# Linear attention ahead of a Mish feed-forward: exponentials by sign in two tiles, num by sign within a bank, loads placed behind projections, first key unit over two pools

## The chip, the cores and the metric

One core of one Trainium2 chip. The metric is the device time of one execution in microseconds (us), taken as the median of several runs.

## The reference

Eight batches of eight heads, 576 tokens, head width 64. Queries and keys are projected to 128 features, the largest absolute value of each row is subtracted, and both signs go through an exponential. The attention is linear: keys and values are summed first, then the queries are multiplied by the sums. Its output is the input of a feed-forward layer with the Mish activation.

```python
def phi(x):
    proj = np.einsum('bhsd,df->bhsf', x, w_phi)
    proj = proj - np.max(np.abs(proj), axis=-1, keepdims=True)
    return np.concatenate([np.exp(proj), np.exp(-proj)], axis=-1)
q_p, k_p = (phi(q), phi(k))
kv = np.einsum('bhsf,bhsd->bhfd', k_p, v)
z = np.sum(k_p, axis=2)
num = np.einsum('bhsf,bhfd->bhsd', q_p, kv)
den = np.einsum('bhsf,bhf->bhs', q_p, z)[..., None] + 1e-06
...
h = x @ w_in
sp = np.where(h > 20.0, h, np.log1p(np.exp(np.minimum(h, 20.0))))
g = h * np.tanh(sp)
return (g @ w_out).astype(np.float32)
```

## The kernel before

The attention is cut into 36 units of 512 columns (a pair of heads at a time), for keys and for queries alike. The feed-forward weights are split meanwhile into high and low words, 16 pieces of them during the attention; the feed-forward itself (from about 272 us on) uses the split parts and seven products per 2x2 block of blocks.

All operations are entered into one list with a time that was written by hand, as `at(time, fn, unit)`, and the program is the list in the order of the times. The time of unit u is `base(u)`, and a beat is 7.341 in those units. The times set only the order in which each engine finds its instructions; the waits between engines follow from the tiles. The engines each work through their own instructions in order, and SyncE (SP) issues all transfers in order.

What a beat does, by engine:

- TensorE (PE): `q_num` (num, 64 records in the trace), `k_sum` (kvps, 64 or 80), `q_turn` (dt, 16 transposes of the centred query projection), `k_proj` (pp_k, 16), and `project_turn`, which mixes the query projection pp_q with the transposes xt0 and xt1 of a finished output x.
- ScalarE (ACT): `q_exp`, four exponentials that read the two dt banks and write e_q; two key exponentials in place; copies of xt, kv and of the denominators r; a cast for the weights.
- VectorE (DVE): row maxima m_k and m_q, the subtractions e_k and e_q, the reciprocal of r, x = num * r in two operations, and for a weight piece the word operations `shift`, `sign` and `scale` (L194, L198, L204).
- GpSimd (POOL): the rest of the weight split. Its `clamp` (L190) stands ahead of `shift`, its `low` (L219) behind `scale`.
- SP: per beat the store of xs (x_spill), the loads kraw, qraw, v and, on some beats, the words of a weight piece and the two spills of a split piece.

Results of PE land in two PSUM pools. `ps_a` holds two projections pp. `ps_b` has four banks that turn by tag: dt0, dt1, xt0, xt1, num0, num1 and kvps all take the next free one. A tile that takes a bank waits for the last reader of the tile that had it. A num bank is filled by 16 matmuls of two row halves: for each j and t, first the exponentials of one sign, then of the other. The query's tile e_q holds both signs (index s); the signed value s=0 overwrites the centred projection. Key and query tiles share one tag e with five buffers.

The first key unit (unit 0) is projected in two cuts, since its second half is loaded later.

Of the kernel before, what the change touches and what calls it, by code (L numbers as in the profile page):

```python
# [8 lines left out]
F32 = mybir.dt.float32  # L9
# [79 lines left out]
def attention_then_mish(ctx, tc, qT, kT, va, w_phi, w_in, w_out, w_out2, out):  # L89
# [200 lines left out]
    def project(raw, name, cuts=(0, 4)):  # L290

        parts = []
        ps = ps_a.tile([P, 2, 4, F], F32, tag="pp", name=f"pp_{name}")
# [32 lines left out]
    def center(parts, name):  # L326
        e = att.tile([P, 2, 2, 512], F32, tag="e", name=f"e_{name}", bufs=5)
        m = att.tile([P, 2, 4], F32, tag="m", name=f"m_{name}", bufs=4)
        to = e[:, :, 0, :].rearrange("p j (n f) -> p j n f", f=F)
# [4 lines left out]
        return e  # L334

# [33 lines left out]
    def k_center(n):  # L369
        k_live[n] = center(k_live.pop(n), f"k_{n}")  # L370
# [40 lines left out]
    def q_load(n):  # L411
        q_live[n] = att.tile([P, 512], F32, tag="qraw", name=f"qraw_{n}", bufs=3)
        nc.sync.dma_start(q_live[n], qT[n // 2, n % 2])
# [9 lines left out]
    def q_center(n):  # L423
        q_live[n] = center(q_live.pop(n), f"q_{n}")
# [7 lines left out]
    def q_sub(n):  # L432
        ps, m = q_live[n]
        e = att.tile([P, 2, 2, 512], F32, tag="e", name=f"e_q_{n}", bufs=5)
        nc.vector.tensor_tensor(e[:, :, 0, :].rearrange("p j (n f) -> p j n f", f=F), ps,
# [3 lines left out]
    def q_turn(n, j):  # L439
# [5 lines left out]
        for jj in range(2):  # L445
            for i in range(4):
                for h in range(2):
                    rows = slice(h * D, (h + 1) * D)
                    nc.tensor.transpose(turned[n, h][:, jj, i], e[rows, jj, 0, i * P:(i + 1) * P], ident[rows, rows])  # L449

    def q_exp(n, h):
        e, ps = q_live[n].rearrange("p j s (i h t) -> p s h j i t", h=2, t=D), turned.pop((n, h))
        for s in range(2):
            nc.scalar.activation(e[:, s, h], ps, AF.Exp, scale=2.0 * s - 1.0)  # L454

    def q_num(n):
        c, g = divmod(n, 2)
        es = q_live.pop(n)
        x = x_live[n] = att.tile([P, 2, 2, P], F32, tag="x", name=f"x_{n}", bufs=3)
# [381 lines left out]
    for u in range(NU):  # L841
# [4 lines left out]
        at(t + (LOAD_AT[0] if u >= LEAD else -11.1), k_load, u)  # L846
        at(t + (LOAD_AT[1] if u > LEAD else V_AT[u]), v_load, u)
# [74 lines left out]
    for i, pc in enumerate(pieces):  # L922
# [10 lines left out]
        if beat:  # L933
            clock = base(2 * i)
            load_at = clock - (15.0 if i > 3 else 13.4)
        at(load_at, weight_load, *pc)
        for delay, op in bits:
            if i == 2 and op in bits_of(bits, 2, 3):
                delay += STEP
            if i == 2 and op in bits_of(bits, 4):  # L940
# [6 lines left out]
        for j, (cost, op) in enumerate(sums):  # L947
# [3 lines left out]
            if pc[1] >= 2 and j in (high, len(sums) - 1):  # L951
                at(clock + (SPILL_AT[j > high and not quiet] if not beat else 1.2 if j == high else 5.25), spill, int(j > high))
# [163 lines left out]
```

## Time and profile before

| | us |
|---|---|
| median of 3 runs | 1009.7 |
| the runs | 1008.92, 1009.7, 1011.41 |
| the profiled execution, its own time | 1010.88 |
| its span in the profile | 1009.1 |
| PE busy in the span | 992.0 |
| DVE busy | 751.3 |
| ACT busy | 504.4 |
| POOL busy | 286.0 |

The profiled execution lies 1.2 us above the median. The attention ends at about 272 us. In the rows, a value in brackets at the end of a line is the idle time of the engine just ahead of it and what ended it; "issue" means that the profile shows nothing that it waited for. PE stands for matmuls and transposes, PEld for their weight loads.

### The profile page before, as it was taken

How to read it: one execution, taken by the hardware profiler on the slowest of the kernel's cores; microseconds unless marked ns; L12 is line 12 of the kernel's file. 1: busy time of each engine (PE TensorE's matmuls, PEld its weight loads, DVE VectorE, ACT ScalarE, POOL GpSimd, SP SyncE). 2: the span in 40 equal slices, each digit the busy share in tenths (PEclk: the TensorE clock that was granted, in tenths of full speed). 3: DMA queues.
4: the chain of work that ended last, by engine and by line, in shares of the span. 5: the costliest groups of instructions: out<-in, count | busy, mean ns of one | idle time of the engine just before them, and what ended most of it. 6: DMA issues, size and time to landing. Idle time of an engine off the chain costs nothing.

```text
span 1009.1 us, 28988 instructions
## 1 busy us (share of the span) xinstructions
PE 992.0 (98%) x12418; PEld 952.1 (94%) x12418; DVE 751.3 (74%) x1168; ACT 504.4 (50%) x904; POOL 286.0 (28%) x267
## 2 busy tenths in 40 slices
PE   8999999999999999999999999999999999999998
PEld 7989999899999999999999999999999999999998
DVE  7999899888557788879985675757575757575755
ACT  5878887787745446454453433333333333333332
POOL 0674455453505253456536010101010101010101
PEclk9999999999999999999999999999999999999999
DMA  6656577775697968898858996868686868686841
GB/s 209 210 184 197 181 234 240 248 247 177 234 384 295 325 245 308 297 327 284 291 201 284 351 346 218 314 220 312 220 314 222 311 222 311 224 309 223 309 168 73
DMA packets 111200, 259.02 MB, mean 257 GB/s; under 512 B 8672, under 2 KB 47328, under 8 KB 109024
## 3 DMA queue, kind: packets, MB, share of 16 engines
q1 hardware_dynamic: 111072, 257.17, 72.1%
q8 instruction: 98, 1.61, 0.7%
q14 instruction: 30, 0.25, 0.1%
HBM read 179.27 MB, written 77.86 MB: 255 GB/s over the span
## 4 chain that ended last, share of the span: by engine, by line
PE 91%; ACT 5%; issue 2%; POOL 1%; DVE 1%; DMA 0%; SPq 0%; DVEq 0%
PE h L580 36%; PE o L732 22%; PE o L709 15%; PE num L340 7%; PE kvps L340 6%; ACT e_q L454 3%; PE dt L449 2%; PE pp_k L300 1%; PE pp_q L309 1%; ACT e_k L374 1%; DMA kraw<-kT 0%; PE pp_q L300 0%; PE xt L491 0%; DVE e_k L332 0%; PE xt L315 0%
## 5 line engine op out<-in xcount | busy, mean ns | idle before, releaser
L580 PE MATMUL h<-xc,win 128*128 128x256 f32 x3024 | 380.4, 283 | 0.0
L580 PEld LDWEIGHTS h<-xc,win 128*128 128x128 f32 x3024 | 373.8, 192 | 4.4
L804 POOL TENSOR_TENSOR part<-part,du 128x512 f32<-128x512 f32 x18 | 23.4, 1297 | 425.8 <-DVE du L794 425.8
L732 PE MATMUL o<-wa,gh 128*128 128x256 f32 x720 | 130.7, 283 | 0.0
L732 PEld LDWEIGHTS o<-wa,gh 128*128 128x128 f32 x720 | 111.8, 192 | 0.0
L709 PE MATMUL o<-wout,gh 128*128 128x512 f32 x432 | 108.2, 392 | 0.0
L612 DVE TENSOR_TENSOR u<-h,u 128x512 f32<-128x512 f32 x72 | 49.5, 688 | 70.1 <-PE h L580 70.1
L732 PE MATMUL o<-wa,gl 128*128 128x256 f32 x360 | 100.7, 283 | 0.0
L732 PE MATMUL o<-wb,held 128*128 128x256 f32 x795 | 95.8, 281 | 0.2 <-DVE du L794 0.2
L732 PEld LDWEIGHTS o<-wb,held 128*128 128x128 f32 x795 | 94.9, 189 | 0.4 <-DVE du L794 0.4
L709 PEld LDWEIGHTS o<-wout,gh 128*128 128x128 f32 x432 | 77.7, 189 | 13.9
L454 ACT ACTIVATE e_q<-dt 128x512 f32<-128x512 f32 x144 | 74.3, 604 | 17.7 <-PE dt L449 17.5
L340 PE MATMUL kvps<-v,e_k 128*64 128x65 f32 (+1 forms) x2560 | 77.4, 222 | 2.4 <-issue 2.1
L340 PEld LDWEIGHTS num<-kv,e_q 128*64 128x64 f32 x2304 | 71.0, 137 | 8.6 <-ACT e_q L454 5.8
L340 PE MATMUL num<-kv,e_q 128*64 128x65 f32 x2304 | 76.2, 223 | 2.9 <-issue 0.9
L628 ACT ACTIVATE sb<-h 128x256 f32<-128x256 f32 x45 | 17.3, 384 | 119.4 <-PE h L580 85.6
L340 PEld LDWEIGHTS kvps<-v,e_k 128*64 128x64 f32 (+1 forms) x2560 | 72.4, 137 | 4.7 <-issue 2.7
L631 ACT ACTIVATE u<-u 128x768 f32<-128x768 f32 x45 | 38.1, 847 | 72.7 <-DVE u L612 72.7
L374 ACT ACTIVATE e_k<-e_k 128x1024 f32<-128x1024 f32 x64 | 67.7, 1057 | 11.5 <-DVE e_k L332 11.1
L667 ACT CAST gh<-sb 128x1024 fp32r<-128x1024 f32 x45 | 47.2, 1050 | 50.4 <-DVE sb L660 50.4
L732 PEld LDWEIGHTS o<-wa,gl 128*128 128x128 f32 x360 | 68.6, 192 | 0.0
L679 DVE TENSOR_TENSOR gl<-sb,gh 128x1024 fp32r<-128x1024 f32 x45 | 61.0, 1357 | 0.7 <-ACT gh L667 0.7
(111 smaller groups left out, 1614.2 us busy)
## 6 DMA issues: line engine op xcount, KB each, us to landing
win<-in_spill SPq DMA_DIRECT2D x44, 896.0 KB, 8.2
xc<-xc_spill SPq DMA_DIRECT2D x63, 512.0 KB, 5.9
xc_spill<-xc SPq DMA_DIRECT2D x56, 512.0 KB, 6.5
wa<-out_spill SPq DMA_DIRECT2D x29, 768.0 KB, 6.2
in_spill<-wst_in SPq DMA_DIRECT2D x24, 448.0 KB, 3.3
v<-va SPq DMA_DIRECT2D x32, 325.0 KB, 4.4
qraw<-qT SPq DMA_DIRECT2D x36, 256.0 KB, 4.0
x_spill<-xs SPq DMA_DIRECT2D x36, 256.0 KB, 3.0
```

Source lines behind the costliest of these rows:

```text
L340: nc.tensor.matmul(ps[rows], lhsT[:, rows], rhs[h], start=start, stop=stop, skip_group_check=True)
L374: nc.scalar.activation(e[:, :, s], e[:, :, 0], AF.Exp, scale=2.0 * s - 1.0)
L449: nc.tensor.transpose(turned[n, h][:, jj, i], e[rows, jj, 0, i * P:(i + 1) * P], ident[rows, rows])
L454: nc.scalar.activation(e[:, s, h], ps, AF.Exp, scale=2.0 * s - 1.0)
L580: nc.tensor.matmul(ps, w, x, start=(i in (0, 2) and m == 0), stop=(m == 5), skip_group_check=True)
L612: nc.vector.tensor_tensor(u[:, 0:3:2] if second(n) else u[:, 1:3], hy, u2.unsqueeze(1).broadcast_to([P, 2, CH]), op=ALU.add)
L631: nc.scalar.activation(u[:, 0:3], u[:, 0:3], AF.Mish)
L667: nc.scalar.copy(gh, u_live[n][4])
L679: nc.vector.tensor_tensor(gl, u_live[n][4], g_live[n]["h"].bitcast(F32), op=ALU.subtract)
L709: nc.tensor.matmul(o_live[s][tt], g[:, 2 * f + which, cols], wout[fp][:, f, k], start=(first and g is gh and f == k == 0), stop=(last and ...
L732: nc.tensor.matmul(ps, g, w, start=(start and k == 0), stop=(stop and k == 2), skip_group_check=True)
L804: nc.gpsimd.tensor_tensor(cross, cross, d_live[s, tau][0].unsqueeze(1).broadcast_to([P, 2, CH]), op=ALU.add)
```

## The change

The queries' exponentials go to two tiles: e0 (three buffers), in which the projection is centred and which then takes s=0 in place, and e1 (two buffers) for s=1. `q_exp` is now called per sign and not per dt bank: first both banks for s=0, then both for s=1. `q_num` runs over the sign outside j and t within a bank. The keys keep the tag e, now with three buffers; qraw and x have two in place of three.

The second cut of the first key unit is projected into two tiles of `ps_b`, one for each j, and centred by two pairs of VectorE operations.

In the table of times: a key load of unit u stands right behind the key projection of unit u-3, a query load right behind the query projection of unit u-2 (each takes the buffer that this projection frees); v loads stand 0.9 earlier, weight words of pieces 5 and on 22.994 ahead of their beat in place of 15.0; the second spill of a piece 3.3 in place of 5.25 behind; `shift` and `sign` of piece 3 one beat later, as those of piece 2; the query projection of unit 33 is 2.2 earlier.

```diff
     def project(raw, name, cuts=(0, 4)):
...
         for a, b in zip(cuts, cuts[1:]):
-            parts.append((a, b, ps))
+            if a:
+                by_j = [ps_b.tile([P, b - a, F], F32, tag="b", name=f"pp{j}_{name}") for j in range(2)]
+            else:
+                ps = ps_a.tile([P, 2, 4, F], F32, tag="pp", name=f"pp_{name}")
+                by_j = [ps[:, j, a:b] for j in range(2)]
+            parts.append((a, b, by_j if a else ps))
...
-                    nc.tensor.matmul(ps[:, j, n], src, w_phi2[rows], start=True, stop=True)
+                    nc.tensor.matmul(by_j[j][:, n - a], src, w_phi2[rows], start=True, stop=True)
...
+    def centered(n):
+        return att.tile([P, 2, 512], F32, tag="e0", name=f"e0_{n}", bufs=3)
...
+            if a:
+                for j in range(2):
+                    nc.vector.tensor_reduce(m[:, j, a:b], ps[j], axis=AX.X, op=ALU.max, apply_absolute_value=True)
+                    nc.vector.tensor_tensor(to[:, j, a:b], ps[j], m[:, j, a:b].unsqueeze(2).broadcast_to([P, b - a, F]),
+                                            op=ALU.subtract)
+                continue
...
-    def q_exp(n, h):
-        e, ps = q_live[n].rearrange("p j s (i h t) -> p s h j i t", h=2, t=D), turned.pop((n, h))
-        for s in range(2):
-            nc.scalar.activation(e[:, s, h], ps, AF.Exp, scale=2.0 * s - 1.0)
+    def q_exp(n, s):
+        if s:
+            q_live[n] = q_live[n], att.tile([P, 2, 512], F32, tag="e1", name=f"e1_{n}", bufs=2)
+        e = (q_live[n][1] if s else q_live[n]).rearrange("p j (i h t) -> p h j i t", h=2, t=D)
+        for h in range(2):
+            ps = turned.pop((n, h)) if s else turned[n, h]
+            nc.scalar.activation(e[:, h], ps, AF.Exp, scale=2.0 * s - 1.0)
...
         for i in range(2):
-            for j in range(2):
-                for t in range(2):
-                    r0 = (2 * c + t) * P
-                    for s in range(2):
-                        halves(num_live[n, i][:, t, j], es[:, j, s, (2 * i + t) * P:(2 * i + t + 1) * P],
+            for s in range(2):
+                for j in range(2):
+                    for t in range(2):
+                        r0 = (2 * c + t) * P
+                        halves(num_live[n, i][:, t, j], es[s][:, j, (2 * i + t) * P:(2 * i + t + 1) * P],
...
-        at(t + (LOAD_AT[0] if u >= LEAD else -11.1), k_load, u)
+        at(base(2) + 6.22 if u == 9 else base(u - 7) + K_AT[0] + 0.01 if u > 9 else t + (LOAD_AT[0] if u >= LEAD else -11.1), k_load, u)
-        at(t + (LOAD_AT[1] if u > LEAD else V_AT[u]), v_load, u)
+        at(t + (LOAD_AT[1] - (0.9 if u > 9 else 0.0) if u > LEAD else V_AT[u]), v_load, u)
...
-        at(t + LOAD_AT[2] - early, q_load, u)
+        at(base(u - 2) + Q_AT[0] + 0.03 if u > 4 else t + LOAD_AT[2] - early, q_load, u)
...
-            at(t + a[0] - early, q_proj, u)
+            at(t + a[0] - early - (2.2 if u == NU - LEAD + 1 else 0.0), q_proj, u)
...
-            load_at = clock - (15.0 if i > 3 else 13.4)
+            load_at = clock - (STEP * 4 - 6.37 if i > 4 else 15.0 if i > 3 else 13.4)
...
-            if i == 2 and op in bits_of(bits, 2, 3):
+            if i in (2, 3) and op in bits_of(bits, 2, 3):
                 delay += STEP
...
-                at(clock + (SPILL_AT[j > high and not quiet] if not beat else 1.2 if j == high else 5.25), spill, int(j > high))
+                at(clock + (SPILL_AT[j > high and not quiet] if not beat else 1.2 if j == high else 3.3), spill, int(j > high))
```

The order of PE, with its waits, at unit 14, a beat in the middle of the attention: the last transposes of xt of unit 13 and num of unit 14 (kv are the sums of keys and values). Before:

```order
L315 MATMUL xt1_13_2780<-ident_76,x_13_2653 128x64 [waits PE_49,Activation_49]
L315 MATMUL xt1_13_2780<-ident_76,x_13_2653 128x64 x3
L340 MATMUL num0_14_2805<-kv_12_2124,e_q_14_2582 64x65 [waits PE_49,Activation_49]
L340 MATMUL num0_14_2805<-kv_12_2124,e_q_14_2582 64x65 x15
L340 MATMUL num1_14_2806<-kv_13_2279,e_q_14_2582 64x65 [waits Activation_49]
L340 MATMUL num1_14_2806<-kv_13_2279,e_q_14_2582 64x65 x15
```

And of the change:

```order
L319 MATMUL xt1_13_2803<-ident_76,x_13_2679 128x64 [waits PE_49,Activation_49]
L319 MATMUL xt1_13_2803<-ident_76,x_13_2679 128x64 x3
L350 MATMUL num0_14_2830<-kv_12_2144,e0_14_2605 64x65 [waits PE_49,Activation_49]
L350 MATMUL num0_14_2830<-kv_12_2144,e0_14_2605 64x65 x7
L350 MATMUL num0_14_2830<-kv_12_2144,e1_14_2798 64x65 x8
L350 MATMUL num1_14_2831<-kv_13_2298,e0_14_2605 64x65 [waits Activation_49]
L350 MATMUL num1_14_2831<-kv_13_2298,e0_14_2605 64x65 x7
L350 MATMUL num1_14_2831<-kv_13_2298,e1_14_2798 64x65 x8
```

In each bank the eight matmuls on e0 now stand ahead of the eight on e1. The waits stand where they stood: num's first matmul still waits for ScalarE, and no row that reads e1 has a wait of its own.

The order of VectorE around piece 3 of the weights (its tiles are w_in_1_1089 before and w_in_1_1103 in the change; e_q and in the change e_5, e_6 are the queries' subtractions). Before:

```order
L435 TENSOR_TENSOR e_q_1172<-pp_q_1068,m_q_1131 128x2x512
L194 TENSOR_SCALAR w_in_1_1089<-w_in_1_1089 128x512
L198 SCALAR_TENSOR_TENSOR w_in_1_1089<-words_in_1_893,w_in_1_1089 128x512
L331 TENSOR_REDUCE m_k_1282<-pp_k_1201 128x8
L332 TENSOR_TENSOR e_k_1281<-pp_k_1201,m_k_1282 128x2x512
L429 TENSOR_REDUCE m_q_1285<-pp_q_1221 128x8
L479 RECIPROCAL r_1288<-r_1288 128x8
L482 TENSOR_TENSOR x_1246<-num_4_1247,r_1288 128x256
L482 TENSOR_TENSOR x_1246<-num_4_1248,r_1288 128x256
L435 TENSOR_TENSOR e_q_1327<-pp_q_1221,m_q_1285 128x2x512
L204 TENSOR_SCALAR t_in_1_1329<-w_in_1_1089 128x512
```

And of the change:

```order
L449 TENSOR_TENSOR e_5_1186<-pp_q_1080,m_q_1145 128x1024
L343 TENSOR_REDUCE m_k_1295<-pp_k_1211 128x8
L344 TENSOR_TENSOR e_k_1294<-pp_k_1211,m_k_1295 128x2x512
L443 TENSOR_REDUCE m_q_1298<-pp_q_1232 128x8
L496 RECIPROCAL r_1301<-r_1301 128x8
L499 TENSOR_TENSOR x_1259<-num_4_1260,r_1301 128x256
L499 TENSOR_TENSOR x_1259<-num_4_1261,r_1301 128x256
L449 TENSOR_TENSOR e_6_1340<-pp_q_1232,m_q_1298 128x1024
L194 TENSOR_SCALAR w_in_1_1103<-w_in_1_1103 128x512
L198 SCALAR_TENSOR_TENSOR w_in_1_1103<-words_in_1_904,w_in_1_1103 128x512
L204 TENSOR_SCALAR t_in_1_1344<-w_in_1_1103 128x512
```

Shift and sign have moved behind the two x and the next subtraction, directly ahead of scale.

The order of SP in a beat in the middle of the attention (x_spill is the store of a finished output, words_in_0 are a weight piece's). Before:

```order
L504 DMA x_spill_88<-xs_2333 128x512
L357 DMA kraw_2434<-kT 128x512
L413 DMA qraw_2438<-qT 128x512
L364 DMA v_2469<-va 128x650
L168 DMA words_in_0_2471<-w_in 128x1024
L504 DMA x_spill_88<-xs_2495 128x512
```

And of the change:

```order
L521 DMA x_spill_87<-xs_2204 128x512
L367 DMA kraw_2327<-kT 128x512
L168 DMA words_in_0_2329<-w_in 128x1024
L425 DMA qraw_2355<-qT 128x512
L521 DMA x_spill_88<-xs_2357 128x512
L374 DMA v_2460<-va 128x650
L367 DMA kraw_2489<-kT 128x512
```

The words of the piece stand a beat earlier, and the load of v comes ahead of that of the keys.

## Rows read from the trace of the kernel before

**Rows 1.** The page: busy time by engine, granted clock in slices, chain by engine.

```profile
PE 992.0 (98%) x12418; PEld 952.1 (94%) x12418; DVE 751.3 (74%) x1168; ACT 504.4 (50%) x904; POOL 286.0 (28%) x267
...
PEclk9999999999999999999999999999999999999999
...
PE 91%; ACT 5%; issue 2%; POOL 1%; DVE 1%; DMA 0%; SPq 0%; DVEq 0%
```

**Rows 2.** Busy time by windows: stretch, length, engines, clock, DMA share, GB/s.

```profile
0.00:310.00 310.00, 296.26 (x7136) 280.37 (x7137) 253.87 (x343) 229.62 (x461) 144.50 (x144) 1.00 0.70 233
```

**Rows 3.** Waits, 30 to 262 us: waiter, releaser; us in total, times, longest.

```profile
PEld num L340 <- ACT e_q L454: 5.5, 21, 0.7
PE dt L449 <- DVE x L482: 2.8, 3, 1.3
PEld kvps L340 <- issue: 2.7, 4, 1.3
...
PEld xt L491 <- issue: 0.2, 1, 0.2
```

**Rows 4.** Timeline of one beat: start, duration, engine, line, work, count, idle before.

```profile
155.05 2.07 ACT L454 ACTIVATE e_q<-dt 128x512 f32<-128x512 f32 x4 [0.92 <-PE dt L449]
...
156.55 0.14 PEld L315 LDWEIGHTS xt<-ident,x 64*128 64x128 f32 x1
...
157.17 1.43 PEld L340 LDWEIGHTS num<-kv,e_q 128*64 128x64 f32 x46 [0.24 <-ACT e_q L454]
```

**Rows 5.** Timeline of PE at the first key unit's sums.

```profile
9.99 2.09 PE L340 MATMUL kvps<-v,e_k 128*64 128x65 f32 x64
```

**Rows 6.** Timelines of DVE, PE and POOL, 40 to 67 us.

```profile
41.03 0.69 DVE L198 SCALAR_TENSOR_TENSOR w_in<-words_in,w_in 128x512 uint32<-128x512 uint32 x1
41.76 0.43 DVE L204 TENSOR_SCALAR t_in<-w_in 128x512 uint32<-128x512 uint32 x1
...
48.43 2.38 POOL L251 TENSOR_TENSOR win<-w_in,win 128x896 fp32r<-128x896 f32 x1 [1.55 <-ACT win L247]
...
48.98 2.13 DVE L204 TENSOR_SCALAR t_in<-w_in 128x512 uint32<-128x512 uint32 x1
...
57.75 0.43 DVE L194 TENSOR_SCALAR w_in<-w_in 128x512 uint32<-128x512 uint32 x1 [0.81 <-POOL w_in L190]
58.21 1.03 DVE L198 SCALAR_TENSOR_TENSOR w_in<-words_in,w_in 128x512 uint32<-128x512 uint32 x1
...
63.19 0.76 DVE L482 TENSOR_TENSOR x<-num,r 128x256 f32<-128x256 f32 x2
...
63.76 0.68 PE L449 MATMUL dt<-ident,e_q 64*128 64x64 f32 x15 [1.27 <-DVE x L482]
...
65.56 1.27 POOL L219 TENSOR_TENSOR t_in<-w_in,t_in 128x512 f32<-128x512 f32 x1 [3.60 <-DVE t_in L204]
```

**Rows 7.** Timelines of SP and PE, 167 to 190 us; instruction queue of the page.

```profile
168.02 1.15 PE L340 MATMUL kvps<-v,e_k 128*64 128x65 f32 x32 [0.76 <-issue]
...
180.01 0.36 SPq L357 DMA_DIRECT2D kraw<-kT  x1
...
182.08 0.38 SPq L168 DMA_DIRECT2D words_out<-w_out  x1
...
182.96 1.44 PE L340 MATMUL kvps<-v,e_k 128*64 128x65 f32 x41 [1.12 <-issue]
...
189.08 1.10 PE L340 MATMUL num<-kv,e_q 128*64 128x65 f32 x31 [0.89 <-issue]
...
q8 instruction: 98, 1.61, 0.7%
```

**Rows 8.** Timelines of PE and ACT, 246 to 254 us.

```profile
248.55 4.03 ACT L454 ACTIVATE e_q<-dt 128x512 f32<-128x512 f32 x8 [0.50 <-PE dt L449]
248.97 1.01 PE L449 MATMUL dt<-ident,e_q 64*128 64x64 f32 x16 [0.48 <-DVE x L482]
...
251.44 2.73 PE L340 MATMUL num<-kv,e_q 128*64 128x65 f32 x86
```

More of the change, by code (lines that the diff above doesn't have):

```diff
@@ L292, in project @@
         parts = []
-        ps = ps_a.tile([P, 2, 4, F], F32, tag="pp", name=f"pp_{name}")
         for a, b in zip(cuts, cuts[1:]):
-            parts.append((a, b, ps))
+            if a:
[4 more added lines that the diff above has]
+            parts.append((a, b, by_j if a else ps))
             for n in range(a, b):
@@ L324, in project_turn, with center @@
         return [(0, 4, ps)]
-    def center(parts, name):
-        e = att.tile([P, 2, 2, 512], F32, tag="e", name=f"e_{name}", bufs=5)
+    def centered(n):
+        return att.tile([P, 2, 512], F32, tag="e0", name=f"e0_{n}", bufs=3)
+    def center(parts, name, e):
         m = att.tile([P, 2, 4], F32, tag="m", name=f"m_{name}", bufs=4)
-        to = e[:, :, 0, :].rearrange("p j (n f) -> p j n f", f=F)
+        to = e.rearrange("p j (n f) -> p j n f", f=F)
         for a, b, ps in parts:
+            if a:
[4 more added lines that the diff above has]
+                continue
             nc.vector.tensor_reduce(m[:, :, a:b], ps[:, :, a:b], axis=AX.X, op=ALU.max, apply_absolute_value=True)
@@ L333, in center @@
                                     m[:, :, a:b].unsqueeze(3).broadcast_to([P, 2, b - a, F]), op=ALU.subtract)
-        return e
     def halves(ps, lhsT, rhs, start, stop):
@@ L369, in k_center @@
     def k_center(n):
-        k_live[n] = center(k_live.pop(n), f"k_{n}")
+        e = att.tile([P, 2, 2, 512], F32, tag="e", name=f"e_k_{n}", bufs=3)
+        center(k_live.pop(n), f"k_{n}", e[:, :, 0, :])
+        k_live[n] = e
     def k_exp(n, s):
@@ L411, in q_load @@
     def q_load(n):
-        q_live[n] = att.tile([P, 512], F32, tag="qraw", name=f"qraw_{n}", bufs=3)
+        q_live[n] = att.tile([P, 512], F32, tag="qraw", name=f"qraw_{n}", bufs=2)
         nc.sync.dma_start(q_live[n], qT[n // 2, n % 2])
@@ L423, in q_center @@
     def q_center(n):
-        q_live[n] = center(q_live.pop(n), f"q_{n}")
+        e = centered(n)
+        center(q_live.pop(n), f"q_{n}", e)
+        q_live[n] = e
     def q_max(n):
@@ L433, in q_sub @@
         ps, m = q_live[n]
-        e = att.tile([P, 2, 2, 512], F32, tag="e", name=f"e_q_{n}", bufs=5)
-        nc.vector.tensor_tensor(e[:, :, 0, :].rearrange("p j (n f) -> p j n f", f=F), ps,
+        e = centered(n)
+        nc.vector.tensor_tensor(e.rearrange("p j (n f) -> p j n f", f=F), ps,
                                 m.unsqueeze(3).broadcast_to([P, 2, 4, F]), op=ALU.subtract)
@@ L448, in q_turn @@
                     rows = slice(h * D, (h + 1) * D)
-                    nc.tensor.transpose(turned[n, h][:, jj, i], e[rows, jj, 0, i * P:(i + 1) * P], ident[rows, rows])
-    def q_exp(n, h):
-        e, ps = q_live[n].rearrange("p j s (i h t) -> p s h j i t", h=2, t=D), turned.pop((n, h))
-        for s in range(2):
-            nc.scalar.activation(e[:, s, h], ps, AF.Exp, scale=2.0 * s - 1.0)
+                    nc.tensor.transpose(turned[n, h][:, jj, i], e[rows, jj, i * P:(i + 1) * P], ident[rows, rows])
+    def q_exp(n, s):
[5 more added lines that the diff above has]
+            nc.scalar.activation(e[:, h], ps, AF.Exp, scale=2.0 * s - 1.0)
     def q_num(n):
@@ L458, in q_num @@
         es = q_live.pop(n)
-        x = x_live[n] = att.tile([P, 2, 2, P], F32, tag="x", name=f"x_{n}", bufs=3)
+        x = x_live[n] = att.tile([P, 2, 2, P], F32, tag="x", name=f"x_{n}", bufs=2)
         for i in range(2):
@@ L934, in attention_then_mish @@
             clock = base(2 * i)
-            load_at = clock - (15.0 if i > 3 else 13.4)
+            load_at = clock - (STEP * 4 - 6.37 if i > 4 else 15.0 if i > 3 else 13.4)
         at(load_at, weight_load, *pc)
         for delay, op in bits:
-            if i == 2 and op in bits_of(bits, 2, 3):
+            if i in (2, 3) and op in bits_of(bits, 2, 3):
                 delay += STEP
-            if i == 2 and op in bits_of(bits, 4):
+            if i in (2, 3) and op in bits_of(bits, 4):
                 delay += 0.05
```

## Prediction

> **What bounds the kernel now.** I read the page first. TensorE (PE) is busy for 98% of the span at the full granted clock in every slice, and 91% of the chain that ended last lies on PE [rows 1]. So time can only come out of the roughly 2% in which PE stands still, or out of stretches where another engine gives PE its work late. The change touches the attention stage alone: there the view by windows counts 296.26 us of PE work in the first 310 us [rows 2]. The feed-forward stage behind it issues the same instructions in the same order in both programs, so I carry it over unchanged.
>
> Next I read PE's waits between 30 and 262 us. The order of the program explains three kinds [rows 3]. First, the transposes of the queries' projections (dt) wait for VectorE's x: 2.8 us in three places. Second, the weight loads of num wait for the queries' exponentials: 5.5 us in 21 beats, a quarter of a microsecond each. Third, "issue", where PE waits for nothing that the profile shows: six groups of weight loads from 2.7 down to 0.2 us, 6.7 us together.
>
> The timeline of one beat shows the second kind [rows 4]. The four exponentials take 2.07 us from 155.05; the last ends at 157.12 and each a little under half a us behind the one before it, so the second near 156.14 and the third near 156.63. The loads of xt end 0.24 before num's first load at 157.17, that is at 156.93. num starts 0.05 behind the fourth exponential.
>
> **Exponentials by sign, num by sign.** The exponential count and sizes stay, and so do num's 64 records; nothing is added there. What could be gained is that num starts on e0 while e1 is still being made, 2 of 4 exponentials earlier. But a num tile is also a PSUM bank, and ps_b has only four. From the order of the built program I followed which tile held each bank before. In 29 of the 36 units num0 takes the bank of dt1, which is read until the fourth exponential in both versions. In these units the first matmul of num0 waits for the fourth exponential as before, and the wait of 0.24 stays. I take 0. Units 4, 13, 22 and 33 take dt0's bank (third exponential), and only units 0, 34 and 35 are really opened. For unit 0 I take -0.2, the wait of one beat.
>
> The swap has a price: dt0's bank is now free after the third exponential and not after the second. xt1 takes that bank. Its first load stood at 156.55 [rows 4] and would stand near 156.67, so xt ends near 157.05 where num may start at 157.12 or later. The slack left is 0.07 at most: no loss, but little cover. If it were gone, each of 29 beats would pay what is over. Bounds: 0 and, if num really opened in all beats, -5.5.
>
> **First key unit over two pools.** It keeps the matmuls and adds two small VectorE operations (four of 256 columns a row in place of two of 512). Behind it the next thing is kvps at 9.99, which starts with no wait [rows 5]. I take 0.
>
> **Piece 3's word operations one beat later.** At 57.75 VectorE waits 0.81 for GpSimd, then does shift and sign (0.43 and 1.03) ahead of the key reduce. Everything behind them is late: x is done from 63.19, and PE's dt waits 1.27 at 63.76 [rows 6]. The change puts both operations behind the next query subtract, directly ahead of their scale. Taken off, 2.27 us come out of VectorE's chain, more than the 1.27 that PE waited, so this gap closes: -1.3. What is late next: the following beat carries three word operations together. An earlier piece did just that, from shift to scale at 41.03 and 41.76, 0.69 and 0.43 each, with no wait of PE behind it. GpSimd, which needs the scale, idled 3.60 there before its multiply at 65.56 [rows 6], so a later scale costs GpSimd and not PE. Bounds: -1.3 and 0. The other two gaps of rows 3 (1.1 and 0.48) have other causes and stay: at 48.98 the scale took 2.13 in place of 0.43 while GpSimd's 2.38 from 48.43 ran [rows 6].
>
> **Loads behind projections.** Before, SP issues a beat's loads in one burst: at 180.01 keys, then queries and values, at 182.08 weight words. PE then stood 1.12 in the middle of a run of kvps, until 182.96, for nothing that the profile shows. The same form stands at 168.02 (0.76, burst from 164.82 to 167.02) and 189.08 (0.89, burst from 187.74) [rows 7]. What is waited for inside a run of equal matmuls whose operands are all there can be little but the instructions themselves; the page has a queue for them, 98 packets of 1.61 MB [rows 7], which shares the DMA engines with the loads. In the order of the change each load waits for the projection that frees its buffer, values come 0.9 and words 8 us earlier, and the second spill stands next to the first: the bursts are spread through the beat, with the same bytes. None of the loads comes late: keys are issued 3 units, queries 2 units ahead. These three stalls make 2.8 of the 6.7 us; I take most of them, -2.5. Bounds: -6.7 (all) and, if the spread loads meet more fetches, the same amount up.
>
> The Trainium skill (Runtime: NRT & Kernel Launch, section Instruction fetch mechanics) speaks against this term. It says that an engine's sequencer refills its instruction buffer in 16 KiB blocks by a queue of its own, and that crossing a block is mostly hidden. The packets agree with the block (1.61 MB over 98 is 16 KiB); the stalls inside runs do not look hidden. By the rule the term is 0 and the sum is that of the first rival.
>
> **Tail.** q_proj of unit 33 moves 2.2 earlier, ahead of dt of unit 31. Before, dt of unit 32 waited 0.48 at 248.97, eight exponentials took 4.03 from 248.55, num of unit 31 began at 251.44 [rows 8]. Sixteen projections ahead of dt31 put its exponentials about 0.9 later, num31 0.1 later, and its second bank up to 0.46 more: +0.4. The opened num in units 33 to 35 gives about -0.4 back. I take 0, between -0.9 and +0.6.
>
> **The sum.** -1.3 (VectorE) - 2.5 (loads) - 0.2 (unit 0) + 0 = -4.0. The profiled execution took 1010.88, so 1006.9 by its own measure; it lies 1.2 above the median of the runs, 1009.7, so the median should become **1005.7**.
>
> **Rivals.** A difference of 0.3% (3.0 us, 1006.7 and 1012.7) is about what this measurement can tell from no change.
> - *Only the program's own waits move.* The issue stalls stay, wherever loads stand. For it: shorter stalls further on follow only one or two issues, not bursts. Against: three of the longest stand in bursts. 1009.7 - 1.3 - 0.2 = 1008.2.
> - *num opens after all.* If the bank that num0 gets were free early in most beats, 5.5 of num's waits go. Against it: the order of banks above. 1009.7 - 1.5 - 5.5 = 1002.7, lower still with the loads' term.
> - *SP becomes a queue that waits (slower).* Each key and query load now waits on PE at the head of SP, and x_spill, spills and words queue behind it. Should these come out together after the wait, bulk traffic is denser than before and the issue stalls double, +6.7: 1009.7 - 1.5 + 6.7 = 1014.9. It decides from +4.5 on, where the gain of 1.5 is spent and 3.0 more. Against: in the new order loads and projections alternate, so each wait is for work that PE is about to do.
> - *The change doesn't do what it says.* The stall moves one beat on: three word operations stand together there (1.54) and GpSimd may stretch one as at 48.98, by 1.7. With no effect of the loads: 1009.7 - 1.3 + 1.3 to 1.7, about 1010.
>
> **Chances.** Forecast 0.48 (its own range 1003.5 to 1008, two thirds of it under 1006.7), only own waits 0.22, num opens 0.12, the stall moves on 0.10, SP waits 0.08. Faster: 0.32 of the forecast, 0.03 of the first rival, 0.12 of the second, 0.47. Same: 0.16 + 0.19 + 0.10, 0.45. Slower: 0.08. The range 1002 to 1011 leaves out SP waiting, the lower part of num opening (0.05) and ends of the forecast.
>
> **What would show it.** In the profile after: dt at about 63 us without a wait on VectorE; num's first load still waiting some 0.24 on the fourth exponential (e1 from dt1) in most beats; xt's first load behind the third exponential without num moving; the issue waits of PE's loads at about 4 in place of 6.7 us; SP's issues spread. I am wrong if num waits for exponentials much less than 5.5 in all, or more; if a new wait of PE stands behind words in the beat after 63 us; or if issue waits stay or grow.

## The result, and the profile after

The changed kernel is slower: 1022.64 us in the median of 6 runs (1015.54 to 1024.96) against 1011.21 for the kernel before (6 runs, 1008.92 to 1016.75). The ratio is 1.0101, with a 95% interval of 1.0072 to 1.0129. The prediction was 1005.7 with a range of 1002 to 1011: wrong, and on the wrong side.

The page after (busy time by engine; chain by engine):

```profile
PE 994.7 (97%) x12418; PEld 954.6 (93%) x12418; DVE 751.4 (73%) x1170; ACT 504.4 (49%) x904; POOL 285.3 (28%) x267
...
PE 96%; issue 2%; DVE 1%; ACT 1%; DMA 0%; SPq 0%; DVEq 0%
```

The instructions are as many as in [rows 1]; two DVE operations came in, as foretold. The time is lost in the attention alone. From the last num to the end of the span both kernels take 738 us. In the first 310 us PE has 284.89 us of work in place of 296.26 [rows 2] (view by windows, columns as there):

```profile
0.00:310.00 310.00, 284.89 (x7047) 270.19 (x7048) 244.47 (x333) 223.67 (x451) 137.21 (x137) 0.99 0.67 214
```

The waits after, 30 to 262 us, answer to [rows 3] (waiter, releaser; us in total, times, longest):

```profile
PEld kvps L350 <- issue: 16.3, 10, 4.3
...
PEld num L350 <- ACT e L471: 3.0, 18, 0.2
PEld pp_k L304 <- issue: 2.1, 3, 0.9
...
PEld num L350 <- issue: 1.1, 2, 0.7
...
PEld pp_q L313 <- issue: 0.5, 1, 0.5
...
PEld dt L463 <- issue: 0.3, 1, 0.3
...
PEld xt L319 <- issue: 0.2, 1, 0.2
```

The six groups of issue waits make 20.5 us where there were 6.7. That is 13.8 us more, about as much as the whole loss: the profiled execution of the change took 1024.96, 14.1 more than that of before. No group of dt that waits for VectorE is left, and num waits less for exponentials, 3.0 in place of 5.5.

The issue waits stand in a pattern. The timeline of PE shows them in kvps of every second beat:

```profile
86.17 0.56 PE L350 MATMUL kvps<-v,e_k 64*64 64x65 f32 x18 [1.65 <-issue]
...
101.50 0.58 PE L350 MATMUL kvps<-v,e_k 64*64 64x65 f32 x24 [1.42 <-issue]
...
116.88 0.81 PE L350 MATMUL kvps<-v,e_k 64*64 64x65 f32 x30 [1.44 <-issue]
```

Each stands behind a burst of SP. For the first of them (num of that beat starts at 80.65):

```profile
79.45 0.33 SPq L367 DMA_DIRECT2D kraw<-kT  x1
79.88 0.37 SPq L168 DMA_DIRECT2D words_out<-w_out  x1
80.62 0.33 SPq L425 DMA_DIRECT2D qraw<-qT  x1
81.16 0.33 SPq L521 DMA_DIRECT2D x_spill<-xs  x1
...
86.67 0.33 SPq L374 DMA_DIRECT2D v<-va  x1
```

Four transfers, 1.31 MB, go out within 2.1 us, and then nothing for 5. The view of transfers, in the window from num's start to 83.75 and in the one after it (queue, packets, MB, share), shows when the instruction packet moved:

```profile
q1 hardware_dynamic: 344, 0.90, 91.3%
...
q1 hardware_dynamic: 185, 0.33, 82.2%
q8 instruction: 1, 0.02, 5.5%
```

In the first 3.1 us 0.90 MB of SP's transfers moved and no packet of instructions; in the next window one moved (at 83.80 in the trace), and PE went on at 86.17.

That these waits are for instructions can be counted. Number all records of PE in the trace (matmuls, loads, semaphore waits; 25109 for 98 packets, 256 a packet) by their starts. From 30 to 272 us, 17 loads waited on issue for more than 0.3 us, 20.3 us together. Every one of them is record 193 or 194 behind a multiple of 256, so all lie at one boundary of a block, and each went on 1.2 to 1.6 us after an instruction packet had ended. PE passed 47 such boundaries there, 30 without such a wait. In the kernel before, 6 of 50 had one. Over all kernels of this document the same place has 266 of 271 such waits.

One longer wait had a second price. PE stood 4.13 us up to 208.11, with no work from 204 to 208, and the granted clock of the next 4 us was 0.63 in the mean, so most of them ran at the lower of the two levels, 1.2 and 2.4 GHz (windows):

```profile
204.00:208.00 4.00, 0.00 (x0) 0.00 (x0) 2.68 (x5) 0.40 (x1) 0.27 (x1) 1.00 0.41 150
208.00:212.00 4.00, 3.89 (x76) 3.70 (x78) 0.00 (x0) 1.62 (x4) 0.00 (x0) 0.63 0.30 93
```

### The profile page after: what moved, and what is told of

Same layout as the page of the kernel before. It is cut to its first block, busy times and chain, and to the rows that moved or that the text cites. A ratio compares the mean times of both kernels' runs of the same rounds, so it can differ in the third digit from the quotient of the medians.

```text
span 1023.2 us, 29010 instructions
## 1 busy us (share of the span) xinstructions
PE 994.7 (97%) x12418; PEld 954.6 (93%) x12418; DVE 751.4 (73%) x1170; ACT 504.4 (49%) x904; POOL 285.3 (28%) x267
## 4 chain that ended last, share of the span: by engine, by line
PE 96%; issue 2%; DVE 1%; ACT 1%; DMA 0%; SPq 0%; DVEq 0%
PE h L597 35%; PE o L749 22%; PE o L726 14%; PE num L350 7%; PE kvps L350 7%; PE pp_k L304 3%; PE pp_q L313 3%; PE dt L463 2%; PE xt L319 1%; PE pp_q L304 1%; DMA kraw<-kT 0%; ACT e L471 0%; PE xt L508 0%; PE z L749 0%; DVE m_k L343 0%
## 5 line engine op out<-in xcount | busy, mean ns | idle before, releaser
L350 PE MATMUL kvps<-v,e_k 128*64 128x65 f32 (+1 forms) x2560 | 79.5, 223 | 15.7 <-issue 15.0
L471 ACT ACTIVATE e<-dt 128x512 f32<-128x512 f32 x144 | 74.2, 603 | 20.9 <-PE dt L463 20.7
L350 PE MATMUL num<-kv,e 128*64 128x65 f32 x2304 | 75.6, 223 | 1.7 <-issue 0.9
L350 PEld LDWEIGHTS num<-kv,e 128*64 128x64 f32 x2304 | 70.4, 138 | 6.5 <-ACT e L471 3.7
L386 ACT ACTIVATE e_k<-e_k 128x1024 f32<-128x1024 f32 x64 | 67.7, 1057 | 10.7 <-DVE e_k L344 10.4
L343 DVE TENSOR_REDUCE m_k<-pp_k 128x8 f32<-128x1024 f32 (+1 forms) x36 | 43.5, 1207 | 31.8 <-PE pp_k L304 31.8
```

Of the source, the lines that this page charges most:

```text
L350: nc.tensor.matmul(ps[rows], lhsT[:, rows], rhs[h], start=start, stop=stop, skip_group_check=True)
L386: nc.scalar.activation(e[:, :, s], e[:, :, 0], AF.Exp, scale=2.0 * s - 1.0)
L471: nc.scalar.activation(e[:, h], ps, AF.Exp, scale=2.0 * s - 1.0)
```

## The experiments

The theory ahead of the first runs: SP's new order puts loads into a burst just where PE asks for its next block of instructions, the block waits behind them, and PE runs dry some 2 us later. The rivals: another part of the change makes the loss, or the size of the bursts alone does. One table has all runs. "Issue" is the sum of PE's weight-load groups that wait on issue from 30 to 272 us in the profiled execution, and "rest" is that execution's own time less this sum. Each ratio compares all runs of a kernel with runs of the kernel before that were taken beside them (medians from 1011.2 to 1013.1), so it is not the quotient of two medians of this table.

| run | own time | issue | rest | median | ratio to before (95%) |
|---|---|---|---|---|---|
| before | 1010.88 | 7.0 | 1003.9 | 1011.21 | 1 |
| the change | 1024.96 | 20.5 | 1004.5 | 1022.64 | 1.0101 (1.0072 to 1.0129) |
| change, old places of loads | 1015.67 | 10.5 | 1005.2 | 1012.12 | 1.0000 (0.9981 to 1.0019) |
| before, new places of loads | 1015.49 | 12.2 | 1003.3 | 1013.53 | 1.0012 (0.9996 to 1.0028) |
| words a beat later | 1016.24 | 13.2 | 1003.0 | 1017.00 | 1.0040 (1.0017 to 1.0063) |
| words behind v | 1020.20 | 14.6 | 1005.6 | 1019.63 | 1.0073 (1.0052 to 1.0095) |
| words behind x_spill | 1017.85 | 14.1 | 1003.8 | 1014.28 | 1.0034 (1.0016 to 1.0052) |
| 32 matmuls of one column more | 1034.01 | 14.4 | 1019.6 | 1036.24 | 1.0238 (1.0214 to 1.0262) |
| 4 matmuls more | 1024.16 | 16.8 | 1007.4 | 1023.43 | 1.0105 (1.0074 to 1.0136) |
| 8 matmuls more | 1025.34 | 17.8 | 1007.5 | 1025.01 | 1.0128 (1.0084 to 1.0172) |
| 16 matmuls more | 1027.70 | 21.7 | 1006.0 | 1021.96 | 1.0081 (1.0063 to 1.0099) |
| 32 matmuls more | 1018.17 | 12.9 | 1005.3 | 1021.75 | 1.0091 (1.0061 to 1.0121) |
| old exponentials and num | 1011.45 | 9.0 | 1002.5 | 1014.14 | 1.0030 (1.0008 to 1.0051) |
| one pool | 1020.34 | 15.9 | 1004.4 | 1021.62 | 1.0094 (1.0076 to 1.0111) |
| word operations of piece 3 as before | 1023.97 | 20.0 | 1004.0 | 1023.32 | 1.0114 (1.0085 to 1.0143) |
| keys behind v, words behind x_spill | 1015.29 | 9.8 | 1005.5 | 1014.72 | 1.0027 (1.0012 to 1.0042) |
| old order of exponentials | 1016.60 | 10.4 | 1006.2 | 1015.11 | 1.0017 (0.9993 to 1.0041) |
| old order of num | 1023.82 | 19.2 | 1004.6 | 1022.86 | 1.0095 (1.0064 to 1.0125) |
| without the words of pieces 6 to 15 | 1018.18 | 14.4 | 1003.8 | 1013.40 | 1.0013 (0.9996 to 1.0031) |
| keys and words moved, old exponentials | 1015.59 | 11.3 | 1004.3 | 1013.20 | 1.0021 (1.0001 to 1.0041) |

The rest lies between 1002.5 and 1006.2 in all runs without added matmuls, while the issue waits go from 7 to 20.5. What tells the kernels apart is the issue waits, and nothing else of size. A single execution scatters by 3 us and more around its median, so medians and ratios decide.

**The loads alone, and all but the loads.** In the change, the old lines of load places (shown for keys and queries; v, words and spills likewise):

```diff
-        at(base(2) + 6.22 if u == 9 else base(u - 7) + K_AT[0] + 0.01 if u > 9 else t + (LOAD_AT[0] if u >= LEAD else -11.1), k_load, u)
+        at(t + (LOAD_AT[0] if u >= LEAD else -11.1), k_load, u)
-        at(base(u - 2) + Q_AT[0] + 0.03 if u > 4 else t + LOAD_AT[2] - early, q_load, u)
+        at(t + LOAD_AT[2] - early, q_load, u)
```

> The changed kernel with every load, weight word and spill back at its old place in SP's order; the rest of the change stays. Theory (late instruction refills behind bursts of loads, set by where the loads stand): the waits of PE's kvps on issue fall from 15.0 us to under 5 and the time to 1008 to 1011. Rival (the split by sign, the two pools or the moved word operations make the loss): 1019 to 1023, issue waits as after.

And the same lines put into the kernel before:

> The kernel before with only the new places of loads, words and spills (and two buffers for qraw). Theory: PE waits on issue in the kvps of every second beat, 12 to 18 us in all, and the time is 1019 to 1023. Rival (other parts make the loss): 1008 to 1011.

The first came as the theory said, 1.0000; the second did not: 1.0012, not to be told from no change. Neither half costs anything measurable and both together cost 1%. So the loads' new places are needed for the loss, but not enough. The stall exists in the second kernel too, but only here and there. In its timeline from 75 to 120 us there is one:

```profile
101.97 0.58 PE L340 MATMUL kvps<-v,e_k 64*64 64x65 f32 x24 [1.86 <-issue]
```

**Weight words at other places.** Three kernels move only the words' load in the change:

```diff
-            load_at = clock - (STEP * 4 - 6.37 if i > 4 else 15.0 if i > 3 else 13.4)
+            load_at = clock - (15.0 if i > 3 else 13.4)
```

> The changed kernel with the loads of weight words one beat later, as before; all else as changed. The words then stand in the other beat of each pair, again between kraw and qraw, so the bursts are as large as after. Theory with a phase (three refills in two beats, one of which is asked for right behind the burst with the words): the waits on issue fall under 7 us, the time to 1010 to 1015. Rival (the burst's size alone decides, not its place against the refills): 12 us or more of issue waits stay, 1019 to 1023.

with `STEP * 3 + 1.76` in place of `STEP * 4 - 6.37`:

> The changed kernel with the weight words right behind the load of v in SP's order, some 2 us ahead of the keys' load instead of between keys and queries; all bytes as changed. Theory (a refill asked for right behind keys and words waits behind their 0.77 MB): its delay falls under 2.5 us, the stall in the kvps of every second beat goes, issue waits 5 to 9 us, time 1008 to 1013. Rival (the burst's size decides): bursts are smaller too, so the same; this run alone does not tell these apart.

and with `STEP * 3 - 1.72`:

> The changed kernel with the weight words right behind the store of x_spill: the same four transfers of 1.28 MB in the same burst of the same beat, only with the words last, behind the time at which the refill is asked for. Theory (order against the refill): the regular stall goes, issue waits 5 to 10 us, time 1008 to 1014. Rival (the burst's size decides): stalls stay, 1019 to 1023.

Measured 1.0040, 1.0073 and 1.0034. The same burst with the words last lost a third of what the change lost, so the order within a burst counts and not its size alone; from 75 to 120 us no stall at all came in that kernel's kvps, one of 1.38 in num. But words behind v, where bursts are smaller, kept most of the loss. None of the three came under the kernel before, and the issue waits stayed at 13 to 15 us in all three, where the theory expected under 7, 5 to 9 and 5 to 10.

**The block boundary moved.** If only the place of the blocks against the bursts counted, extra matmuls in the first key unit, which shift each later block by so many records, should change the loss. Four counts were tried, 32 (below), 16, and later 8 and 4, and ahead of them 32 of one column each (`by_j[0][:, 0, 0:1], w_phi2, w_phi2[:, 0:1]`):

```diff
                 by_j = [ps_b.tile([P, b - a, F], F32, tag="b", name=f"pp{j}_{name}") for j in range(2)]
+                for i in range(32):
+                    rows = slice(i % 2 * D, i % 2 * D + D)
+                    nc.tensor.matmul(by_j[0][rows, 0, 0:VW], w_phi2[:, rows], w_phi2[:, 0:VW], start=True, stop=True,
+                                     skip_group_check=True)
```

> The changed kernel with 32 small matmuls of one column more in the first key unit, where PE waits for a load: 128 more records of PE, half an instruction block, so that every later refill is asked for half a block earlier against the loads; they cost 1 to 2 us themselves. Theory with a phase: the stall in the kvps of every second beat goes or becomes under half, issue waits under 8 us, time 1011 to 1017. Rival (burst's size alone): issue waits stay at 15 us, time 1022 to 1026.

> The changed kernel with 16 matmuls of 64x65 more in the first key unit (64 records, a quarter of an instruction block, about 1 us, while PE waits there for a load): every later refill is asked for a quarter block, some 1.2 us, earlier. Theory with order: the refill is asked for ahead of the words, the stall of every second beat goes or is halved; issue waits 7 to 13 us, time 1010 to 1016. Rival (size of burst): 1022 to 1025.

> As the run with 32 small matmuls, but with matmuls of 64x65 that take 2 us and not 10 (128 records, half a block). The earlier run spent 10 us on them and kept 14 us of issue waits at other places of the beat. Theory with order: issue waits 10 to 15 us again, time 1013 to 1019; rival (size of burst): 1022 to 1026.

The 32 matmuls of one column took 14 us by themselves (not 10, as the expectation above has it), which puts that run out of the comparison:

```profile
4.36 13.81 PE L297 MATMUL pp_k<-head 128*128 128x1 f32 x64
```

With 16 and 32 proper ones the ratio stayed, 1.0081 and 1.0091, of which 1 to 2 us are the added matmuls. The stalls moved, though. With 32 they stand mostly outside kvps (waits, 30 to 272 us):

```profile
PEld dt L467 <- issue: 4.0, 3, 1.9
PEld pp_q L317 <- issue: 3.6, 5, 1.2
PEld pp_k L308 <- issue: 3.4, 3, 1.5
PEld kvps L354 <- issue: 1.4, 1, 1.4
```

So moving the boundary moves where PE runs dry, and does not by itself end it. A beat takes about a block and a half (384 records of matmuls and loads, at 256 to a block), so of the three blocks in two beats it is likely that one meets a burst somewhere.

**Parts of the change undone, one at a time.** The split of exponentials and num, the two pools, the move of piece 3, each with the loads at their new places:

The split undone (both diffs of the next paragraph):

> The changed kernel with the exponentials and num in the old order (by dt bank, sign innermost), the two tiles e0 and e1 and all else as changed. Theory (issue waits make the time; the split adds nothing by itself): the time less the issue waits stays at 1003 to 1006; num's waits for exponentials go back from 3.0 to about 5 us; the time, where the refills meet the loads as they happen to, 1010 to 1022. Rival (the split by sign costs time itself): the time less the issue waits falls by 5 or more, to under 1000.

One pool (and without the two pairs of VectorE operations):

```diff
-            if a:
-                by_j = [ps_b.tile([P, b - a, F], F32, tag="b", name=f"pp{j}_{name}") for j in range(2)]
-            else:
+            if not a:
                 ps = ps_a.tile([P, 2, 4, F], F32, tag="pp", name=f"pp_{name}")
-                by_j = [ps[:, j, a:b] for j in range(2)]
-            parts.append((a, b, by_j if a else ps))
+            by_j = [ps[:, j, a:b] for j in range(2)]
+            parts.append((a, b, ps))
```

> The changed kernel with the first key unit in one pool again (one wait less in PE's instructions, one load of work a little later). Theory: 0 by itself; time less issue waits 1003 to 1007. As the beats start some 1 us later against nothing else that is fixed, 1015 to 1024. Rival (the first unit's early start lets the refills and loads meet): 1010 to 1014.

Piece 3 as before:

```diff
-            if i in (2, 3) and op in bits_of(bits, 2, 3):
+            if i == 2 and op in bits_of(bits, 2, 3):
...
-            if i in (2, 3) and op in bits_of(bits, 4):
+            if i == 2 and op in bits_of(bits, 4):
```

> The changed kernel with shift and sign of piece 3 in their old beat. By the prediction 1.3 us slower by a wait of dt for VectorE's x near 63 us, so time less issue waits 1005 to 1007. Rival (the move costs itself): time less issue waits under 1003, no wait of dt on VectorE lost.

One pool and the old place of piece 3 leave the loss, 1.0094 and 1.0114. The old exponentials and num take most of it away, 1.0030. The split's own cost in the rest cannot be told from scatter (1002.5 without it, 1004.5 with it); what it changes is the issue waits. Without the move of piece 3, the wait of dt is back, and small:

```profile
PE dt L463 <- DVE x L499: 0.7, 1, 0.7
```

**Which half of the split.** One kernel takes the old order of the exponentials and keeps num by sign, the other the reverse:

```diff
-    def q_exp(n, s):
+    def q_exp(n, h):
...
-        for h in range(2):
-            ps = turned.pop((n, h)) if s else turned[n, h]
-            nc.scalar.activation(e[:, h], ps, AF.Exp, scale=2.0 * s - 1.0)
+        ps = turned.pop((n, h))
+        for s in range(2):
+            e = q_live[n][s].rearrange("p j (i h t) -> p h j i t", h=2, t=D)
+            nc.scalar.activation(e[:, h], ps, AF.Exp, scale=2.0 * s - 1.0)
```

```diff
-            for s in range(2):
-                for j in range(2):
-                    for t in range(2):
+            for j in range(2):
+                for t in range(2):
+                    for s in range(2):
```

> The changed kernel with the exponentials in the old order (both signs of dt0, then of dt1), num still by sign. Theory (xt1's wait for the third exponential holds PE's sequencer ahead of the refill): the regular stall near 85, 100 and 115 us goes, issue waits 7 to 12, time 1010 to 1015. Rival (num's order does it): 1019 to 1024.

> The changed kernel with num's old order (sign innermost), exponentials still by sign. Theory: the stall of every second beat stays, issue waits 14 to 21, time 1018 to 1024. Rival (num's order does it): 1010 to 1015.

1.0017 and 1.0095: it is the order of the exponentials. With num's old order the pattern of the change is there, stall by stall (timeline of PE):

```profile
86.51 0.56 PE L350 MATMUL kvps<-v,e_k 64*64 64x65 f32 x18 [1.65 <-issue]
...
102.13 0.58 PE L350 MATMUL kvps<-v,e_k 64*64 64x65 f32 x24 [1.69 <-issue]
...
118.32 0.81 PE L350 MATMUL kvps<-v,e_k 64*64 64x65 f32 x30 [2.26 <-issue]
```

With the old exponentials no stall stands between 75 and 120 us. The same beat as above in the kernel with the old exponentials, first PE, then SP, then the transfers from 86.7 to 87.8:

```profile
85.79 2.09 PE L350 MATMUL num<-kv,e 128*64 128x65 f32 x64
87.71 2.20 PE L350 MATMUL kvps<-v,e_k 128*64 128x65 f32 x80
```

```profile
84.60 0.33 SPq L367 DMA_DIRECT2D kraw<-kT  x1
85.03 0.38 SPq L168 DMA_DIRECT2D words_out<-w_out  x1
85.77 0.33 SPq L425 DMA_DIRECT2D qraw<-qT  x1
86.31 0.81 SPq L521 DMA_DIRECT2D x_spill<-xs  x1
```

```profile
q1 hardware_dynamic: 119, 0.41, 98.1%
q8 instruction: 1, 0.02, 5.6%
```

Against num's start the four issues stand as in the change: 1.19, 0.76 and 0.02 ahead and 0.52 behind here, 1.20, 0.77 and 0.03 ahead and 0.51 behind there. But the instruction packet moves 0.98 us after num's start (86.77 in the trace) and not 3.15. All 80 records of kvps run through.

The block that PE lacks in the change can be compared in all three beats with a stall above, also with a kernel that does not load these words (below). The table, counted from the traces, has the start of the block's packet behind the start of PE's record at the boundary one block earlier, and how many of the words' 128 packets had started by then.

| kernel | packet behind the boundary, us | words' packets started |
|---|---|---|
| the change | 3.47, 3.40, 3.76 | 128, 128, 128 |
| old order of exponentials | 1.36, 1.97, 2.12 | 8, 38, 24 |
| without the words of pieces 6 to 15 | 1.35, 1.83, 1.89 | none |

In the change the block came only when all packets of the words had started. With the old exponentials it came among them, nearly as early as without words.

**On which side of the wait?** One explanation was tried at the boundary: xt1 waits for the third and not the second exponential, this holds PE's instruction stream for some tenths, and the request for the block lies just behind that wait. Then a few records more would carry it to the other side; the edit is the one above with 4 and with 8 matmuls.

> The changed kernel with 4 matmuls of 64x65 more in the first key unit (16 records, 0.2 us): the place in the program at which PE asks for a block moves 16 records ahead, from behind xt1's wait to ahead of it. Theory: the stall of every second beat goes, issue waits 7 to 13, time 1010 to 1016. Rival (only distances of 1 us and more count, not the side of the wait): 1020 to 1024 as the changed kernel.

> The same with 8 matmuls (32 records, 0.5 us). Theory: as with 4, 1010 to 1016. Rival: 1020 to 1024.

It fell: 1.0105 and 1.0128 (1023.43 and 1025.01 us), the rival's values or a little above.

**The words' bytes taken away.** The words of pieces 6 to 15 are not loaded, the exponentials stay by sign:

```diff
...
+        i = pieces.index((kind, fp, k))
+        if 5 < i < EARLY:
+            piece[kind, fp, k] = [kept[0].rearrange("p (a b) -> p b a", b=2)]
+            return
...
```

> The changed kernel without the loads of weight words of pieces 6 to 15: all these pieces are split from the words of piece 5, kept in a tile, so the weights are wrong and ten transfers of 512 KB are gone; all engines do the same work, exponentials and loads otherwise as changed. Theory (the late blocks wait behind the words' bytes): the stalls of 1.5 us and more in the kvps of every second beat go, issue waits 4 to 9 us, time 1007 to 1013. Rival (the third exponential holds PE's sequencer, whatever the transfers are): issue waits 14 to 20 us, time 1018 to 1024.

The median fell to 1013.40, 1.0013. The profiled execution was the slowest of that kernel's ten (1011.47 to 1018.18), and its 14.4 us of issue waits are more than expected, mostly ahead of 75 us, where words are still loaded, and behind 135 us. But the stalls of every second beat are gone; in the stretch where the change had three of 1.42 to 1.65 there is this alone (timeline of PE, 84 to 122 us):

```profile
104.07 0.58 PE L360 MATMUL kvps<-v,e_k 64*64 64x65 f32 x24 [0.23 <-issue]
```

So in these beats it is behind the words' bytes that the blocks waited, and the third exponential by itself holds nothing up there. The waits ahead of 75 and behind 135 us lie at block boundaries too; behind 135 us they come without words, and what held those blocks was not looked into.

**Other placings.** Keys behind v and words behind x_spill, with the new and with the old order of the exponentials:

```diff
-        at(base(2) + 6.22 if u == 9 else base(u - 7) + K_AT[0] + 0.01 if u > 9 else t + (LOAD_AT[0] if u >= LEAD else -11.1), k_load, u)
+        at(base(2) + 6.22 if u == 9 else base(u - 6) - 1.76 if u > 9 else t + (LOAD_AT[0] if u >= LEAD else -11.1), k_load, u)
-            load_at = clock - (STEP * 4 - 6.37 if i > 4 else 15.0 if i > 3 else 13.4)
+            load_at = clock - (STEP * 3 - 1.72 if i > 4 else 15.0 if i > 3 else 13.4)
```

> The changed kernel with keys loaded right behind v, a beat later than in the change, and weight words behind the store of x: two bursts a beat, of 0.58 and 0.5 or 1.0 MB, some 2.5 us apart. Theory (a refill waits for what stands ahead of it in the transfers): refills later than 2.5 us become fewer than 6, issue waits 4 to 9 us, time 1007 to 1012. Rival (spreading never helps, since more refills meet some load): issue waits 12 or more, time over 1014.

> The changed kernel with the exponentials in the old order (num by sign), the keys' loads behind v and the weight words behind the store of x: the two best placings so far in one. Theory: issue waits 6 to 9 us, 1008 to 1012, at or a little below the kernel before. Rival (some blocks always meet loads as long as these fill 70% of the transfer time): 1012 to 1016, no better than either alone.

1.0027 and 1.0021. Both are far better than the change, and neither beats the kernel before. In the first the issue waits, 9.8 us, lie between theory and rival; in the second, 11.3 us and 1013.20 are the rival's, whose reading, that some blocks always meet loads, fits better. No version here does beat it.

## Why the prediction was wrong, point by point

**Loads behind projections, -2.5: the step that failed.** The sentence "the bursts are spread through the beat" is refuted by SP's rows: the key projection, the query projection and xt stand next to each other on PE, so loads gated by them come out together, 1.31 MB within 2.1 us with the words in their midst, then nothing. SP's longest wait from 30 to 272 us is now that of the keys' load on PE; before, it was that of the store on its copy xs (waits of SP, before and after):

```profile
SPq L504 <- ACT xs L501: 105.5, 30, 6.3
...
SPq L367 <- PE xt L319: 76.9, 24, 6.5
```

I read the order of SP and did not set it against the times at which its gates open. The issue waits, which this term was to lower by 2.5, measured +13.5 (7.0 to 20.5 us over 30 to 272 us). Of that, the new places alone make 5.2 in the kernel before (12.2 us); the rest needs the new order of the exponentials as well. The view that it rests on was right: the waits inside equal runs are for instructions, which queue behind loads. The rival of a waiting SP queue had the mechanism and a price of +6.7, half the real one, and I gave it 0.08; its +4.5, from which it decides, was passed by far. The rule of the Trainium skill (Runtime: NRT & Kernel Launch, section Instruction fetch mechanics), by which crossing a block is mostly hidden, holds here for most crossings and not for the time: 30 of 47 boundaries in the change show no wait over 0.3 us, the other 17 cost 20 us, and such waits make nearly the whole difference between the kernels.

**The split by sign, 0 in the beats: right by itself, wrong in company.** num's first loads still wait for the fourth exponential in most beats, 18 times in place of 21, and the waits are shorter (3.0 in place of 5.5, most often 0.17 in place of 0.24 a beat) only since xt ends later, as foretold: num still starts 0.05 behind the exponential. The wait was to stay at 5.5, and much less was named as a sign of being wrong; but with num's old order it is 2.9 and with the old exponentials 5.2 (30 to 262 us), so num by sign opened nothing. But "no loss, but little cover" priced xt's delay on PE alone. With the loads at their new places, the order of the exponentials decides whether the block waits behind the words, 1.0017 against 1.0095. What in that order does it is open. SP's issues agree within some hundredths of a us, and the words' first packets within 0.3 us (0.97, 1.21 and 1.67 us behind the boundary in the change, 1.26, 1.35 and 1.69 with the old exponentials). The explanation by the side of xt1's wait fell.

**Piece 3's word operations, -1.3: right in the trace.** Shift, sign and scale stand together and run without a stretch, and dt of this beat, at 61.09, has no wait (DVE, then PE, after):

```profile
62.00 0.42 DVE L194 TENSOR_SCALAR w_in<-w_in 128x512 uint32<-128x512 uint32 x1
62.45 0.69 DVE L198 SCALAR_TENSOR_TENSOR w_in<-words_in,w_in 128x512 uint32<-128x512 uint32 x1
63.17 0.43 DVE L204 TENSOR_SCALAR t_in<-w_in 128x512 uint32<-128x512 uint32 x1
```

```profile
61.09 0.71 PE L463 MATMUL dt<-ident,e 64*128 64x64 f32 x16
```

The kernel without the move shows 0.7 of the wait back; in its total time this is below what can be told. The other two gaps, which I let stand, went too: in place of the one of 1.1 us PE stood 0.78 us on issue just ahead of that dt, and the one of 0.48 in the tail is gone, as q_proj stands there now.

**First key unit over two pools, 0: a little too careful.** Its kvps starts at 8.57 in place of 9.99 [rows 5], and num of unit 1 at 35.00 in place of 36.13, so about 1 us is gained in these two executions:

```profile
8.57 2.09 PE L350 MATMUL kvps<-v,e_k 128*64 128x65 f32 x64
```

The total of the kernel with one pool (1.0094) cannot be told from the change's, so this rests on the traces alone. There the kernel with one pool starts at 9.29, and kernels with two pools start at 9.07 to 9.61 when other parts are undone, so how much of it the pools give is not shown.

**Tail, 0: right.** From the first record of num of unit 30 to the start of the last the change takes 25.39, the kernel before 25.16.

**The sum.** The rest after is 1004.5 against 1003.9, where -1.5 to -2.5 was due. By an estimate, about 1.3 us of that is the slow clock after the long wait (76 records in the 4 us at 0.63, where the 4 us from 196 had 113); the remainder is within the scatter of single executions.

## What to carry to other kernels

When transfers are tied to the work that frees their buffers, look up when those gates open on the clock: gates that open together make a burst. In a program with few waits on PE, add up the "issue" waits first. They are a resource with a queue of its own, and a change that moves loads or shifts a wait by tenths can move them by more than all the dependencies it improves. Two edits that each measure as nothing may cost 1% together, so measure them in the pair in which they will run.

## What was not expected of the hardware

- Instruction blocks wait behind loads. In the change a block started 3.15 us after num's start, when 0.90 MB of SP's transfers had moved; in the kernel with the old exponentials it started 0.98 us after it, with loads issued at the same times to 0.02 us.
- All 17 issue waits over 0.3 us that the change shows from 30 to 272 us lie at the same place in a count of 256 records. So the program fixes where PE can run dry, and the transfers decide whether it does.
- After a wait of 4.13 us PE's granted clock was 0.63 over the next 4 us and 0.95 over the 4 after.
- A matmul of one column with 128x128 weights took 0.216 us a record (64 in 13.81), against 0.033 for the 64x65 matmuls of num (64 in 2.09).
